# Two held-back second-layer pieces move ahead of the last block's projections

## Chip, cores and metric

One Trainium2 chip, one core. The metric is the device time of one execution in microseconds (us); the figure for a kernel is the median of its runs.

## The reference

One transformer block with adaptive layer norm, one sequence of 2048 rows of 576 numbers, 32 heads of 18:

```
mod = silu(c) @ w_mod                      # six vectors sa, ca, ga, sb, cb, gb
h = layernorm(x) * (1 + ca) + sa
x = x + ga * (softmax(q k^T * 18**-0.5) v) @ wo       # q, k, v = h @ wqkv
h = layernorm(x) * (1 + cb) + sb
x = x + gb * silu(h @ w1) @ w2             # hidden width 4608
```

All inputs and the output are float32.

## The kernel before

The rows are cut into four blocks of 512 (`b` = 0 to 3), and a block into four row tiles of 128 (`j` = 0 to 3). TensorE runs attention block after block; what follows attention in a block, called here its second half, is done while the attention of the next block runs. For the last block there is no next attention: its second half is the tail of the kernel, in which TensorE has nothing else to do. Every product is split into a high and a low part, so that one product is three matmul passes.

`post(b)` (line 1059) writes down the second half of a block as a list of items in the order in which TensorE is to run them: each `fl.add` appends one. TensorE's order is exactly this list's; the other engines' orders (VectorE is DVE, ScalarE ACT, GpSimd POOL, and SyncE, or SP, which issues all transfers named here) are made by a scheduler that walks the same program with a model of durations. So a change in the list can also change the order on DVE and on SP. An engine, SP among them, works through its own order strictly: whatever stands behind a waiting instruction waits too.

The second half of a block is, in order:

1. `o_T` (line 1067): the attention output `ou` is split into `th` and `tl`.
2. The output projection, `proj` (line 1089), row tile after row tile: 28 matmuls of 128x288 into two banks `psp`, one bank per half of the 576 columns. Its weights `wo` lie in the buffers that later hold the first four `w1t` and one `w2t`. When a row tile's two halves are done, `add_x1` (line 1105) adds each bank to the residual tile `x` on DVE (line 1108).
3. The layer norm of that row tile, in four steps (`ln_steps`, line 1143): statistics (lines 1121, 1125, 455), the reciprocal root (line 457 on POOL, lines 463 to 467 on DVE), and the scaling into `ob` (line 471), of which POOL copies a last piece (line 472). For row tile j these steps are strewn among the projections of row tile j + 1; for the last row tile (j = 3) there is no next projection, and they come in the loop at line 1194.
4. `h_T` (line 1146): 20 transposes of `ob` by TensorE (`psT`, line 1157), five column tiles kt of four row tiles each. In the last block they come as 15 transposes of row tiles 0 to 2 and then 5 of row tile 3. From each `psT` bank ACT makes `eq` (line 475) and DVE makes `hh` (line 478), and `hl` = `eq` - `hh` (line 485) on DVE for even kt and on POOL for odd kt.
5. The two layers of the MLP: `mlp1` (line 1234, `ps`<-`hh`,`w1t`, 128x512), and `mlp2` (line 1267, `ps`<-`w2t`,`g`, 128x288), whose results DVE adds to the residual tile; a row tile that has its last addition goes to the output (line 1287).

**Held-back pieces.** Block 2 doesn't finish its second layer before block 3's second half begins: its last four hidden tiles' share of `mlp2` is kept as a list `left` of 32 pieces of three matmuls each. `rest(n)` (line 1173) puts the next n of them into the list of the running block, as work for TensorE while others are busy. The 32 pieces in their order: 16 for the row tiles 0 and 1 of block 2, 8 for row tile 2 (12 matmuls per column half), 8 for row tile 3. After a row tile's last piece DVE adds its second half, and the row tile is written out.

For block 3 `LREST` (line 60) says how many pieces stand ahead of the projections of each row tile, the loop at line 1194 puts two ahead of each of the four layer norm steps of the last row tile, and a `rest(99)` behind the transposes takes what is left.

**The residual tiles.** Residual tiles share five buffers (`x1`, `bufs=5`, line 1056). Block 2 holds four of them until they are written out; block 3's four loads (line 1057) take the fifth buffer and then those of block 2's row tiles 0, 1 and 2, in this order. So the load of block 3's residual tile 3 has to wait until block 2's row tile 2 has been written out.

In the rows below, `x_23433`, `x_23435`, `x_23437`, `x_23439` are block 2's residual tiles 0 to 3; `x_30924`, `x_30926`, `x_30928`, `x_30930` are block 3's.

Of the kernel before, what the change touches and what calls it, by code (L numbers as in the profile page):

```python
# [56 lines left out]
END = -4  # L57
END0 = 40
LP0 = 1000
REST, LREST = (16, 8, 0, 0), (22, 0, 0, 0)  # L60
LP = 8000
PB = 9
ORDER = (
# [346 lines left out]
def tile_adaln_block(ctx: ExitStack, tc: tile.TileContext, x, wqkv, wo, w1, w2, c, ccol, wfirst, wcol, out):  # L410
# [589 lines left out]
    def out_b(i, ov):  # L1000

        b, qd = divmod(i, NQUAD)
        if qd == 0:
            if b:
                fill.until("h_T")
            o[b] = att.tile([P, KT, QB], F32, tag="o", name="ou", bufs=1)
        ou = o[b]
        tt = ou[:, 4, :]
        nc.vector.transpose(tt, ov)
        blocks = tt.rearrange("p (b c) -> p b c", c=32)  # L1010
        rec = att.tile([P, 16], F32, name="rec", bufs=2)
        nc.vector.reciprocal(rec, blocks[:, :, DH])
        nc.vector.tensor_tensor(blocks[:, :, :DH], blocks[:, :, :DH], rec[:, :, None].to_broadcast([P, 16, DH]), op=ALU.mult)
        nc.vector.transpose(ov, tt)
        o["at", b] = None
        chain([("V", 700), ("V", 260), ("V", 460), ("V", 700)], plan.t + 700, None, lambda at: o.update({("at", b): at + (5500 if b else 6500)}))
        for h in range(4):
            for kt, r0, d0, d1 in head_rows(4 * qd + h):
                nc.sync.dma_start(ou[r0:r0 + d1 - d0, kt, :], ov[32 * h + d0:32 * h + d1, :])
        del quads[i]  # L1020
        if qd == NQUAD - 1:
            post(b)
# [36 lines left out]
    def post(b):  # L1059
# [5 lines left out]
        last = state["tail"] = plan.off = b == NQB - 1  # L1065
# [51 lines left out]
        def ln_stat(j, n):  # L1117
            if n == 0:
                c["st", j] = pool.tile([P, 2, 6], F32, name="st6", bufs=3), pool.tile([P, 1, 2], F32, name="mv2", bufs=4)
            st6, mv = c["st", j]  # L1120
            nc.vector.bn_stats(st6[:, n, :], c["x1"][j][:, n * HH:(n + 1) * HH])
            if n == 0:
                plan.op("V", plan.t, 450)
                return
            nc.vector.bn_aggr(mv[:, 0, :], st6)
            c["v", j] = rstd_a(pool, mv, 1)
            c["ve", j] = Event(plan)
            c["x", j].then(lambda at: chain([("V", 450), ("V", 330), ("G", 560)], at, None, c["ve", j].set))

        def ln_rs(j):  # L1130
            c["rs", j] = rstd_b(pool, *c["v", j], 1)
            state["ln"] = False
            c["rs_at", j] = Event(plan)
            c["ve", j].then(lambda at: plan.op("V", at, 770, c["rs_at", j].set))

        def ln_c(j):
            if j == 0:
                c["ob"] = att.tile([P, NST, 640], F32, tag="o", name="ob", bufs=1)
            ln_apply(c["x1"][j], c["ob"][:, j, :], c["st", j][1][:, 0, :], c["rs", j], nc.vector)
            c["ln", j] = Event(plan)  # L1140
            c["rs_at", j].then(lambda at: chain([("V", 540), ("G", 240)], at, None, c["ln", j].set))

        def ln_steps(j):
            return [lambda: ln_stat(j, 0), lambda: ln_stat(j, 1), lambda: ln_rs(j), lambda: ln_c(j)]
# [28 lines left out]
        def rest(n):  # L1173
            for _ in range(min(n, len(left))):
                fl.add(*left.pop(0))
# [9 lines left out]
        for j in range(NST):  # L1185
            rest((REST if not last else LREST)[j])
            steps_ = dict(zip((1, 4, 8, 11), ln_steps(j - 1))) if j else {}
            for part in range(len(GP)):
# [2 lines left out]
                    fl.add(0, lambda i=part // 3: w2_load(i))  # L1191
                if part in steps_:
                    fl.add(0, steps_[part])
        for step in ln_steps(3):
            if b == 0:
                fl.add(700)
            rest(2)
            fl.add(0, step)
        if not last:
            rest(99)  # L1200
# [563 lines left out]
    step = 0  # L1764
# [101 lines left out]
```

## Time and profile before

| | us |
|---|---|
| runs | 2343.11, 2345.21, 2345.0 |
| median | 2345.0 |
| profiled execution, its own time | 2344.63 |
| span of the instructions in its profile | 2342.8 |
| TensorE (PE) matmuls busy, and weight loads (PEld) | 2288.0 and 1581.4 |
| VectorE (DVE) busy | 1764.1 |
| ScalarE (ACT) busy | 1472.2 |
| GpSimd (POOL) busy | 707.8 |

The span runs from the first instruction to the last; the execution's own time has 1.83 us around it. The profile's times are counted from the start of the span. The tail, from the last attention matmul on, begins at 2064.9 and is 278 us long, about an eighth of the span. TensorE is busy in 98% of the span, so what it can gain lies in the places where it waits; "busy" also hides the times at which its granted clock is below full.

### The profile page before, as it was taken

Reading aid. Unit: us, or ns where it says so; the run is one execution under the profiler, and the core shown is the slowest. Engines: PE = TensorE matmul, PEld = TensorE weight load, DVE = VectorE, ACT = ScalarE, POOL = GpSimd, SP = SyncE. Lnnn points to the kernel's source line nnn. Section 1 sums busy time; section 2 is a strip of 40 time slices with the busy share of each in tenths; the row PEclk is TensorE's granted clock in tenths of the full one; section 3 lists DMA queues with packets and bytes.
Section 4 is the critical chain, followed back from the end, with each engine's and each line's share of the span. In section 5 each row is a group of like instructions: output and inputs, shape, how many; then the busy total and the mean of one; then the engine's idle time right before and its main releaser. Section 6 shows DMA issues by size and latency. Waiting matters only on the chain.

```text
span 2342.8 us, 52324 instructions
## 1 busy us (share of the span) xinstructions
PE 2288.0 (98%) x19954; PEld 1581.4 (67%) x19954; DVE 1764.1 (75%) x3080; ACT 1472.2 (63%) x2712; POOL 707.8 (30%) x856
## 2 busy tenths in 40 slices
PE   7999999999899999999999999999999999979999
PEld 6974444444576766776676777667677777668998
DVE  7788899987788888877888888778887787244333
ACT  4347777776577777766677777666777677722121
POOL 4213333316556666765311111122211111110000
PEclk9999999998999999999999999999999999999999
DMA  7555555446556666665655545564555554345553
GB/s 277 175 173 177 181 182 175 158 151 198 187 196 216 212 226 219 220 227 189 219 168 178 173 167 166 177 197 167 183 165 172 186 186 161 110 169 178 218 204 120
DMA packets 201619, 433.55 MB, mean 185 GB/s; under 512 B 31506, under 2 KB 67762, under 8 KB 201370
## 3 DMA queue, kind: packets, MB, share of 16 engines
q1 hardware_dynamic: 201370, 430.21, 55.3%
q8 instruction: 159, 2.61, 0.5%
q14 instruction: 90, 0.74, 0.1%
HBM read 339.07 MB, written 86.33 MB: 182 GB/s over the span
## 4 chain that ended last, share of the span: by engine, by line
PE 89%; DVE 4%; DMA 3%; ACT 1%; POOL 1%; issue 1%; SPq 0%; DVEq 0%; ACTq 0%; POOLq 0%
PE ps L560 27%; PE psv L991 19%; PE psa L902 14%; PE ps L554 10%; PE psb L954 9%; PE psqk L666 3%; DVE mx L904 2%; PE psv L560 1%; PE psp L560 1%; PE psqk L560 1%; PE psv L1552 1%; PE psp L554 1%; DMA ka<-kscr 1%; DMA raw<-in_w 1%; PE psqk L1552 1%
## 5 line engine op out<-in xcount | busy, mean ns | idle before, releaser
L904 DVE TENSOR_REDUCE mx<-psa 128x1 f32<-128x512 f32 x2048 | 1330.0, 685 | 279.5 <-PE psb L954 170.4
L956 ACT ACTIVATE pt<-psb 128x512 f32<-128x512 f32 x2048 | 1148.2, 599 | 469.3 <-PE psb L954 306.0
L954 PE MATMUL psb<-qt,kb 56*128 56x512 f32 x2048 | 743.5, 421 | 4.5 <-ACT pt L956 4.5
L902 PE MATMUL psa<-ka,qt 54*128 54x512 f32 x2016 | 732.9, 417 | 11.0 <-DVE mx L904 9.1
L902 PEld LDWEIGHTS psa<-ka,qt 54*128 54x128 f32 x2016 | 347.9, 186 | 304.3 <-DVE mx L904 168.4
L991 PE MATMUL psv<-pt,vt 128*32 128x512 f32 x4096 | 512.2, 606 | 0.3 <-ACT ov L995 0.3
L560 PE MATMUL ps<-w2t,g 64*128 64x288 f32 x4992 | 412.5, 293 | 1.6 <-POOL w2t L787 1.0
L560 PEld LDWEIGHTS ps<-w2t,g 64*128 64x128 f32 x4992 | 384.8, 185 | 42.2 <-DVE x L1108 6.0
L954 PEld LDWEIGHTS psb<-qt,kb 56*128 56x128 f32 x2048 | 351.8, 186 | 29.0 <-ACT pt L956 18.1
L560 PE MATMUL ps<-hh,w1t 64*128 64x512 f32 x1944 | 351.5, 394 | 0.0
L1264 POOL TENSOR_TENSOR g<-etmp,g 128x512 fp32r<-128x512 f32 x108 | 137.8, 1296 | 386.9 <-ACT g L1263 349.6
L991 PEld LDWEIGHTS psv<-pt,vt 128*32 128x32 f32 x4096 | 102.5, 109 | 212.2 <-issue 204.5
L560 PEld LDWEIGHTS ps<-hh,w1t 64*128 64x128 f32 x1944 | 193.9, 186 | 44.0 <-ACT etmp L1260 3.4
L1115 POOL TENSOR_TENSOR x<-x,gt 128x288 f32<-128x288 f32 x116 | 92.9, 801 | 388.1 <-ACT gt L1114 383.3
L560 PE MATMUL ps<-hl,w1t 64*128 64x512 f32 x864 | 177.4, 391 | 0.0
L1108 DVE TENSOR_TENSOR x<-ps,x 128x288 f32<-128x288 f32 x184 | 83.1, 453 | 105.0 <-PE ps L554 69.8
L554 PE MATMUL ps<-w2t,g 128*128 128x288 f32 x960 | 130.2, 296 | 0.0
L554 PEld LDWEIGHTS ps<-w2t,g 128*128 128x128 f32 x960 | 129.1, 189 | 1.5 <-issue 0.8
L1260 ACT ACTIVATE eq<-ps 128x512 f32<-128x512 f32 x36 | 21.5, 600 | 146.6 <-PE ps L554 146.6
L554 PE MATMUL ps<-hh,w1t 128*128 128x512 f32 x360 | 107.1, 391 | 0.0
L560 PEld LDWEIGHTS ps<-hl,w1t 64*128 64x128 f32 x864 | 88.4, 186 | 15.2
L1261 DVE SCALAR_TENSOR_TENSOR etmp<-etmp 128x512 f32<-128x512 f32 x108 | 75.8, 742 | 11.8 <-ACT etmp L1260 10.9
(157 smaller groups left out, 2126.5 us busy)
## 6 DMA issues: line engine op xcount, KB each, us to landing
w1t<-w1s SPq DMA_DIRECT2D x108, 640.0 KB
w2t<-w2s SPq DMA_DIRECT2D x108, 576.0 KB
kb<-kscr SPq DMA_DIRECT2D x512, 108.0 KB
ka<-kscr SPq DMA_DIRECT2D x504, 108.0 KB
w1s<-w1t SPq DMA_DIRECT2D x36, 640.0 KB
w2s<-w2t SPq DMA_DIRECT2D x36, 576.0 KB
vt<-vscr SPq DMA_DIRECT2D x32, 608.0 KB
qt<-qscr SPq DMA_DIRECT2D x128, 108.0 KB
```

Of the source, the lines that this page charges most:

```text
L554: mm(self.ps[late], lhsT=lhsT, rhs=rhs, start=(i == 0), stop=(i == self.n - 1))
L560: done = mm(self.ps[g], lhsT=lhsT[rows], rhs=rhs[rows], start=(s == 0), stop=(s == self.end))
L666: mm(qk_ps[0], lhsT=w[b][:, kt, :], rhs=(hTl if a else hTh)[:, kt, n * 512:(n + 1) * 512], start=(i == 0), stop=(i == 13))
L902: mm(ps, lhsT=t["q"][64 * j:64 * j + 54, hp, stt * P:(stt + 1) * P], rhs=t["a" if ("a", kc, hp) in t else "b", kc, hp][64 * j:64 * j + 54, ...
L904: return lambda: nc.vector.tensor_reduce(t["mx"][:, 2 * j + hp, stt, kc:kc + 1], ps, axis=AX.X, op=ALU.max)
L954: state["pe"] = mm(ps, lhsT=t["b", kt // 4, hp][64 * e:64 * e + 56, kt % 4 * P:(kt % 4 + 1) * P], rhs=t["q"][64 * e:64 * e + 56, hp, :], s ...
L956: nc.scalar.activation(t["P"][kt, hp][:, e, :], ps, AF.Exp, scale=SCALE)
L991: mm(t["ps"][32 * h:32 * h + 32, :], lhsT=t["v"][:, c0:c0 + 32], rhs=t["P"][kt, h // 2][:, h % 2, :], start=(kt == 0), stop=(kt == NKT - 1 ...
L1108: nc.vector.tensor_add(c["x1"][j][:, hs], ps, c["x1"][j][:, hs])
L1115: nc.gpsimd.tensor_add(c["x1"][j][:, hs], c["x1"][j][:, hs], t)
L1261: nc.vector.scalar_tensor_tensor(t, t, 1.0, u, op0=ALU.add, op1=ALU.mult)
L1264: (nc.vector if last else nc.gpsimd).tensor_tensor(g[:, 1, :], t, f(g[:, 0, :]), op=ALU.subtract)
```

## The change

```
-REST, LREST = (16, 8, 0, 0), (22, 0, 0, 0)
+REST, LREST = (16, 8, 0, 0), (24, 0, 0, 0)
...
-        for step in ln_steps(3):
+        for n, step in enumerate(ln_steps(3)):
             if b == 0:
                 fl.add(700)
-            rest(2)
+            rest(1 if last and n else 2)
             fl.add(0, step)
```

For the last block, 24 of the 32 pieces stand ahead of the projections instead of 22. Ahead of the last row tile's four layer norm steps stand 2, 1, 1 and 1 pieces, five in all; before there were 2 each, which is eight by the code and by the order (the change's own words say seven). Behind the transposes three pieces are left instead of two: 24 + 5 + 3 = 32, as 22 + 8 + 2 before. No instruction of TensorE is added or taken away.

On TensorE, the stretch from the end of the last projection (`psp`) to the first layer of the MLP; `ps_31031` is the second column half of block 2's row tile 2, `ps_31242` and `ps_31243` (now `ps_31239` and `ps_31240`) the halves of its row tile 3:

```order
 L554 MATMUL psp<-wo_30920,tl 128x288
 L554 MATMUL psp<-wo_30922,th 128x288 x2
-L554 MATMUL ps_31031<-w2t,g 128x288 x6
-L554 MATMUL ps_31242<-w2t,g 128x288 x12
-L554 MATMUL ps_31243<-w2t,g 128x288 x6
+L554 MATMUL ps_31239<-w2t,g 128x288 x12
+L554 MATMUL ps_31240<-w2t,g 128x288 x3
 L1157 MATMUL psT<-ident,ob 128x128 x20
-L554 MATMUL ps_31243<-w2t,g 128x288 x6
+L554 MATMUL ps_31240<-w2t,g 128x288 x9
```

The six last matmuls of `ps_31031` have gone from here to the place ahead of the first projection; 15 matmuls are left between the last projection and the transposes where 24 were, and 9 instead of 6 stand behind the transposes.

On SP, the transfers from the loads of the residual tiles 1 and 2 of block 3 to the writing of block 2's last row tile; `w1t` and `w2t` are the weights of the MLP's first hidden tiles:

```order
 L1057 DMA x_30926<-in_x 128x576
 L1057 DMA x_30928<-in_x 128x576
+L1287 DMA out<-x_23437 128x576
+L1057 DMA x_30930<-in_x 128x576
 L744 DMA w1t<-w1s 128x1280 x4
-L744 DMA w2t<-w2s 128x1152
-L1287 DMA out<-x_23437 128x576
-L744 DMA w2t<-w2s 128x1152 x2
-L1057 DMA x_30930<-in_x 128x576
-L744 DMA w2t<-w2s 128x1152 x2
+L744 DMA w2t<-w2s 128x1152 x5
 L1287 DMA out<-x_23439 128x576
```

The writing of block 2's row tile 2 and the load of block 3's residual tile 3 stood behind the four `w1t` loads, and now stand ahead of them.

On DVE, the additions around the last row tile's layer norm, before:

```order
L471 TENSOR_SCALAR ob<-x_30928,mv_31188,rs 128x576
L1108 TENSOR_TENSOR x_23437<-ps_31031,x_23437 128x288
L1108 TENSOR_TENSOR x_23439<-ps_31242,x_23439 128x288
L1108 TENSOR_TENSOR x_30930<-psp,x_30930 128x288 x2
L1121 BN_STATS st_31239<-x_30930 128x6 x2
L1125 BN_AGGR mv_31240<-st_31239 128x2
L455 TENSOR_SCALAR ve<-mv_31240 128x1
```

and now:

```order
L1108 TENSOR_TENSOR x_30930<-psp,x_30930 128x288
L471 TENSOR_SCALAR ob<-x_30928,mv_31197,rs 128x576
L1121 BN_STATS st_31247<-x_30930 128x6
L1125 BN_AGGR mv_31248<-st_31247 128x2
L1108 TENSOR_TENSOR x_23439<-ps_31239,x_23439 128x288
L455 TENSOR_SCALAR ve<-mv_31248 128x1
```

The two additions to `x_30930` no longer stand behind the additions of block 2's pieces: the first comes while the last projections run (ahead of these rows), the second is the first row here. The addition of `ps_31239` now stands within the last row tile's layer norm, and in the same way that of `ps_31240` now stands between the first two `hh` (line 478) and the first `hl` (line 485), where before one `hh` and one `hl` more stood ahead of it. The second addition to `x_23437`, which was in the rows of before, now follows line 1087, ahead of the first addition to `x_30924`.

## Prediction

> **What bounds the kernel now.** I read first the chain of waits in order of time, cut to the tail (start, length, what). Outside the tail it is TensorE almost throughout and the change touches nothing there; in the tail it leaves TensorE for 17 us:
>
> ```profile
> 2064.86 8.95 PE ps L554 x66
> 2073.81 14.86 PE psp L554 x112
> 2088.66 0.81 PE ps L554 x6
> ...
> 2089.49 0.47 DVE x L1108
> ...
> 2089.98 8.93 DMA out<-x
> ...
> 2098.97 3.48 DMA x<-in_x
> ...
> 2102.53 0.82 DVE x L1108 x2
> ...
> 2106.58 1.33 PE psT L1157 x5
> 2107.91 231.49 PE ps L554 x1374
> ```
>
> The 66 matmuls are the 22 pieces ahead of the projections, the 112 the projections. The six at 2088.66 finish block 2's row tile 2; its addition, its writing (8.93 us) and then the load of the last residual tile into the same buffer (3.48 us) follow one another, and only then can the last layer norm begin. Behind 2107.91 the chain is TensorE to the end, so what is won ahead of that is won at the end.
>
> Next the timeline of TensorE over the same place (start, length, line; in brackets idle time and what ended it):
>
> ```profile
> 2088.50 3.35 PE L554 MATMUL ps<-w2t,g 128*128 128x288 f32 x24
> 2091.68 1.47 PE L1157 MATMUL psT<-ident,ob 128*128 128x128 f32 x12
> 2103.13 0.88 PE L1157 MATMUL psT<-ident,ob 128*128 128x128 f32 x3 [9.98 <-DVE x L1108]
> 2106.58 1.33 PE L1157 MATMUL psT<-ident,ob 128*128 128x128 f32 x5 [2.58 <-DVE ob L471]
> 2107.56 1.79 PE L554 MATMUL ps<-w2t,g 128*128 128x288 f32 x6
> 2109.15 1.05 PE L554 MATMUL ps<-hh,w1t 128*128 128x512 f32 x2
> 2110.09 0.80 PE L554 MATMUL ps<-hl,w1t 128*128 128x512 f32 x1
> 2111.54 0.62 PE L554 MATMUL ps<-hh,w1t 128*128 128x512 f32 x2
> 2112.22 0.62 PE L554 MATMUL ps<-hh,w1t 128*128 128x512 f32 x2
> ```
>
> TensorE has idled 9.98 + 2.58 us here. It is also slow afterwards: six matmuls of 128x288 take from 2107.56 to 2109.15, 0.265 us each, against 8.95 / 66 = 0.135 in the chain. The windows view says why (third number from the end: granted clock):
>
> ```profile
> 2094.00:2096.00 2.00, 0.00 (x0) 0.00 (x0) 0.00 (x0) 0.00 (x0) 0.00 (x0) 1.00 1.00 300
> 2096.00:2098.00 2.00, 0.00 (x0) 0.00 (x0) 0.00 (x0) 0.00 (x0) 0.00 (x0) 0.84 0.99 392
> 2098.00:2100.00 2.00, 0.00 (x0) 0.00 (x0) 0.00 (x0) 0.00 (x0) 0.00 (x0) 0.50 1.04 424
> 2110.00:2111.00 1.00, 1.00 (x3) 0.81 (x3) 1.00 (x3) 0.78 (x1) 1.00 (x1) 0.50 0.92 359
> 2111.00:2112.00 1.00, 1.00 (x6) 0.77 (x5) 1.00 (x3) 0.78 (x1) 0.18 (x1) 1.00 0.84 327
> ```
>
> The last transposes before the wait end at 2091.68 + 1.47 = 2093.15. A mean of 0.84 over 2096 to 2098 puts the fall to 0.50 at about 2097.4, 4.2 us later. The clock is back at about 2111, 4.4 us after work resumed at 2106.58.
>
> **The change, step by step.** Times stay on the axis of before.
>
> *Pieces ahead.* Two pieces are 6 x 0.135 = 0.81 us, so the last projection ends at 2088.66 + 0.81 = 2089.47. That alone is a shift and no cost: the same matmuls are missing later.
>
> *The residual load.* When does the last residual tile arrive now? DVE and SP of before:
>
> ```profile
> 2075.82 0.68 DVE L1087 TENSOR_TENSOR th<-ou,th 64x512 fp32r<-64x512 f32 x1 [2.32 <-ACT th L1082]
> ```
>
> ```profile
> 2073.79 0.88 SPq L1287 DMA_DIRECT2D out<-x  x2
> 2075.97 1.13 SPq L1057 DMA_DIRECT2D x<-in_x  x2
> 2087.22 2.07 SPq L744 DMA_DIRECT2D w1t<-w1s  x4
> ```
>
> The 24th piece ends at 2073.81 + 0.81 = 2074.6, but its addition stands behind line 1087 on DVE: 2076.5 + 0.46 = 2077.0. The round trip that follows is bounded by two measured ones: a row tile written without a crowd let SP go on after 2075.97 - 2073.79 = 2.18 us; behind the weights it took 8.93. I take 2.18, since the first weights follow only at 2087.22. With 3.48 for the load the tile is there at 2082.7; with 8.93, at 2089.4. The first addition needs it when the first half of the last projection is done, 14.86 / 8 = 1.86 us ahead of 2089.47, at 2087.6. So the wait goes wholly by the first price, and comes back by 1.8 us at most by the second. SP waits in this round trip, and the four `w1t` stand behind it: until 2079.2, or 2085.9 by the dear price, while their buffers come free at 2087.22 + 0.81 = 2088.03. Nothing waits for that.
>
> *The last layer norm.* What is late next is this chain. Row tile 2's layer norm in before shows it without a DMA wait, with the `ob` of the row tile before it in between, as it will now be for row tile 3:
>
> ```profile
> 2084.99 0.46 DVE L1108 TENSOR_TENSOR x<-psp,x 128x288 f32<-128x288 f32 x1 [0.28 <-PE psp L554]
> 2085.36 0.57 DVE L471 TENSOR_SCALAR ob<-x,mv,rs 128x576 f32<-128x576 f32 x1
> ...
> 2086.33 0.21 DVE L1125 BATCH_NORM_AGGREGATE mv<-st 128x2 f32<-128x12 f32 x1
> 2086.58 0.15 DVE L455 TENSOR_SCALAR ve<-mv 128x1 f32<-128x1 f32 x1
> ...
> 2088.16 0.58 DVE L471 TENSOR_SCALAR ob<-x,mv,rs 128x576 f32<-128x576 f32 x1
> ...
> 2107.91 1.53 DVE L478 TENSOR_SCALAR hh<-psT,modc 128x512 fp32r<-128x512 f32 x2 [1.38 <-ACT eq L475]
> 2109.35 0.68 DVE L485 TENSOR_TENSOR hl<-eq,hh 128x512 fp32r<-128x512 f32 x1
> ```
>
> From the addition to the end of `ob`: 2088.16 + 0.58 - 2084.99 = 3.75 us. The inserted addition can start when 12 matmuls of `ps_31239` are done, 2089.47 + 12 x 0.135 = 2091.09, just as DVE comes free (2089.50 + 1.34 + 0.21 = 2091.05); the next instruction starts 0.37 later (as from 2084.99 to 2085.36), so line 455 starts at 2091.48, where it could have at 2091.09: 0.39 us. `ob` ends at 2089.50 + 3.75 + 0.39 = 2093.64. Meanwhile TensorE has 15 matmuls (2.03 us) and 15 transposes at (1.47 - 0.27) / 11 = 0.109 us, taking 0.27 as one's own length (1.64 us): busy to 2093.14. The last five transposes start at 2093.69, with 0.55 us of idling.
>
> *From the transposes to the first layer.* ACT:
>
> ```profile
> 2107.10 2.12 ACT L475 ACTIVATE eq<-psT,modc 128x512 f32<-128x512 f32 x3 [31.31 <-PE psT L1157]
> ```
>
> In before ACT followed the first transpose by 0.52 us at half clock; at full clock I take 0.35 (an estimate: the transpose itself halves from about 0.5 us). So `eq` at 2094.04, `hh` 0.81 later at 2094.85 (as 2107.10 to 2107.91), and `hl` 1.44 after that (2107.91 to 2109.35) plus 0.37 for the addition of `ps_31240` now ahead of it: 2096.66, done 0.68 later at 2097.34, and its matmul 0.06 behind (2110.03 to 2110.09): 2097.40. TensorE has ready work ahead of that only to 2096.11: five transposes to 2094.24, nine matmuls to 2095.46, two on `hh` from 2095.66 (2094.85 + 0.81) at 0.227 us, from (2112.22 - 2111.54) / 3. So 0.20 and 1.29 us of idling stay at this place. The moved piece behind the transposes is covered by this same wait and costs nothing; without that cover it would cost 0.41.
>
> *The clock.* From the first `hl` matmul to the one that starts at 2111.54 in before are four matmuls in 1.45 us; at full clock 4 x 0.227 = 0.91. That is 0.54 us more, if the clock stays up. The idle stretches left, 0.55, 0.20 and 1.29 us, are all shorter than the 2.85 us from 2093.15 to 2096.00 that left the clock at 1.00.
>
> [...]
>
> *Weights.* In before the first `w1t` had 22 us to arrive (2087.22 to 2109.15); now they are needed at 2095.66, 7.6 after their issue. The sizes, from the list of transfers:
>
> ```profile
> w1t<-w1s SPq DMA_DIRECT2D x8, 640.0 KB
> w2t<-w2s SPq DMA_DIRECT2D x5, 576.0 KB
> ...
> out<-x SPq DMA_DIRECT2D x4, 288.0 KB
> ```
>
> In before the written row tile, with four `w1t` and one `w2t` ahead of it, landed at 2098.91, 11.7 us after the first `w1t` was issued. If transfers are served one after another, the first two are there after 1280 / 3424 of that, 4.4 us: at 2092.4, no cost. If all progress together, as late as 2099.7, and the `hl` matmul waits to 2099.7 + 0.45, 2.75 us later. I take the first: the written tile was the last issued and landed last, which speaks for service in turn.
>
> **Sum.** 2110.09 - 2097.40 = 12.69 us, and 0.54 for the clock: 13.2 us. The profiled execution's 2344.63 becomes 2331.4 and its span 2342.8 becomes 2329.6. The median of the three runs is 0.4 us above the profiled execution: 2345.0 - 13.2 = 2331.8.
>
> **Rivals.**
>
> *The clock falls again.* Three short idle stretches within 4 us might count as one. Against it: each is under the 2.85 us that did no harm. For it: nothing here shows several together. Price: 4.4 us at half clock, half of it lost, 2.2 us: 2334.0. [...]
>
> *The weights become the wait*, as priced: 13.2 - 2.75 = 10.5 us of gain, 2334.5.
>
> *Slower.* The load now ahead of `w1t` on SP stalls the weights: SP doesn't issue them until the row tile is written. This decides only if the writing takes more than 2088.03 - 2077.0 = 11 us, and the kernel is slower by 0.2% only if it takes 11 + 13.2 + 4.7 = 29 us: 2349.7 or more. The dearest writing seen here is 8.93, in a crowd that isn't there at 2077.
>
> *The change doesn't do what it says*, that is, the load doesn't come earlier, or a wait as long takes its place: 2345. The order of SP speaks against the first; for the second I find no candidate but the weights.
>
> **How the numbers follow.** The forecast has 0.80, the clock rival 0.07, the weights rival 0.07, no gain 0.04, slower 0.02. The first three are faster. About 0.2% (4.7 us) is what a measurement of this kernel can tell from no change. Faster 0.94, within 0.2% 0.04, slower 0.02. The low end: in before, TensorE needed 30 x 0.135 + 20 x 0.109 + 6 x 0.227 = 7.6 us for what it did between 2088.66 and 2111.54, so at most 22.9 - 7.6 = 15.3 us can go: 2329.7, and 0.7, a third of the 2.1 us between the runs shown, for the spread: 2329.0. The high end takes in either milder rival, and the same 0.7: 2335.2.
>
> **What would show it.** Right: SP writes a row tile near 2077 and loads one near 2079; DVE shows no wait for a residual load; TensorE waits about 0.6 us for `ob` of row tile 3 and about 1.3 for the first `hl`; granted clock 1.00 from 2090 to 2110; first `hl` matmul near 2097.4; span near 2329.6. Wrong: a long wait of DVE for the load, a clock of 0.50 after 2095, TensorE waiting for `w1t`, or the first `hl` matmul after 2100.

## The result, and the profile after

The changed kernel takes 2332.2 us (median of 6 runs, 2329.92 to 2338.06) where the kernel before, measured beside it, takes 2345.14 (6 runs, 2343.11 to 2347.39). The ratio is 0.9947, with a 95% interval of 0.9934 to 0.9961: 9.1 to 15.5 us won. The profiled execution of the changed kernel happens to be its slowest, 2338.06 us with a span of 2336.3, so it stands only 6.6 us below the profiled execution of before. The chain of waits shows why its total misleads (start, length, what):

```profile
2068.81 9.74 PE ps L554 x72
2078.55 14.86 PE psp L554 x112
2093.41 1.61 PE ps L554 x12
...
2097.00 0.59 DVE ob L471
...
2097.63 0.34 PE psT L1157
...
2098.00 0.79 ACT eq L475
...
2098.82 1.53 DVE hh L478 x2
2100.34 0.36 DVE x L1108
2100.71 1.54 DVE hl L485
...
2102.29 230.53 PE ps L554 x1366
...
2332.85 0.46 DVE x L1108
```

The tail, from the first piece ahead of the projections to the last addition, begins at 2068.81, where it began at 2064.86 before: 3.95 us were lost ahead of it, in code that is the same in both. The tail itself lasts 2333.31 - 2068.81 = 264.50 us, against 275.02 (2064.86 to 2339.88) before. So 10.5 us are won in the tail. The two DMA rows of the chain, writing and load, are gone, and what stands between the last projection and the first layer now is the layer norm alone: the addition of `ps_31239` that now stands inside it, `ob`, transposes, `eq`, `hh`, the addition of `ps_31240`, `hl`.

In the queue of SP the order is the new one (start, length, line):

```profile
2079.93 1.13 SPq L1057 DMA_DIRECT2D x<-in_x  x2
2081.16 0.38 SPq L1287 DMA_DIRECT2D out<-x  x1
2085.64 0.33 SPq L1057 DMA_DIRECT2D x<-in_x  x1
2091.97 2.25 SPq L744 DMA_DIRECT2D w1t<-w1s  x4
```

The row tile is written from 2081.16, and 4.48 us later its buffer is loaded with the last residual tile; both stand ahead of the weights. DVE's list of waits over 2060 to 2120 no longer has a row of `x` waiting for `in_x`. Before, it had one of 11.0 us (us in total, times, longest):

```profile
DVE x L1108 <- DMA x<-in_x: 11.0, 1, 11.0
```

TensorE's timeline over the same place (in brackets idle time and what ended it):

```profile
2097.63 0.77 PE L1157 MATMUL psT<-ident,ob 128*128 128x128 f32 x5 [0.59 <-DVE ob L471]
...
2102.29 0.51 PE L554 MATMUL ps<-hl,w1t 128*128 128x512 f32 x1 [1.88 <-DVE hl L485]
2102.64 0.63 PE L554 MATMUL ps<-hh,w1t 128*128 128x512 f32 x2
...
2103.49 1.05 PE L554 MATMUL ps<-hh,w1t 128*128 128x512 f32 x2
```

Of the idle stretches of 9.98 and 2.58 us there remain 0.59 and 1.88. But two matmuls of 128x512 take 0.63 us at 2102.64 and 1.05 at 2103.49. The windows say what that is (third number from the end: granted clock):

```profile
2102.00:2103.00 1.00, 0.71 (x3) 0.62 (x4) 0.96 (x3) 0.65 (x1) 0.00 (x0) 1.00 1.02 419
2103.00:2104.00 1.00, 1.00 (x5) 0.76 (x4) 1.00 (x2) 0.80 (x2) 0.00 (x0) 0.57 1.04 429
2104.00:2105.00 1.00, 1.00 (x4) 0.81 (x3) 1.00 (x2) 0.00 (x0) 0.51 (x1) 0.50 1.05 410
...
2106.00:2107.00 1.00, 1.00 (x5) 0.76 (x4) 0.32 (x1) 0.00 (x0) 0.00 (x0) 0.72 1.05 394
```

By the means of 0.57 and 0.72 the clock falls to a half at 2103.14 and is back at 2106.56: 3.4 us, after the idling is over and with TensorE busy all the time.

### The profile page after: what moved, and what is told of

It reads as the page before. It is cut to its first block, busy times and chain, and to the rows that moved or that the text cites. A ratio compares the mean times of both kernels' runs of the same rounds, so it can differ in the third digit from the quotient of the medians.

```text
span 2336.3 us, 52325 instructions
## 1 busy us (share of the span) xinstructions
PE 2288.4 (98%) x19954; PEld 1584.9 (68%) x19954; DVE 1764.9 (76%) x3080; ACT 1472.7 (63%) x2712; POOL 707.6 (30%) x856
## 4 chain that ended last, share of the span: by engine, by line
PE 87%; DVE 5%; DMA 3%; POOL 1%; ACT 1%; issue 1%; SPq 0%; DVEq 0%; ACTq 0%; POOLq 0%
PE ps L560 27%; PE psv L991 19%; PE psa L902 14%; PE ps L554 10%; PE psb L954 8%; PE psqk L666 3%; DVE mx L904 2%; DMA raw<-in_w 1%; PE psp L560 1%; PE psv L560 1%; PE psv L1552 1%; PE psp L554 1%; DMA qt<-qscr 1%; PE psqk L560 1%; PE psqk L1552 1%
## 5 line engine op out<-in xcount | busy, mean ns | idle before, releaser
L1261 DVE SCALAR_TENSOR_TENSOR etmp<-etmp 128x512 f32<-128x512 f32 x108 | 74.6, 730 | 11.8 <-ACT etmp L1260 10.9
```

Of the source, the lines that this page charges most:

```text
L1261: nc.vector.scalar_tensor_tensor(t, t, 1.0, u, op0=ALU.add, op1=ALU.mult)
```

## The experiments

The theory is that of the prediction: the last residual tile comes into the buffer of block 2's row tile 2, and the 24th piece is the one that frees it early; the whole gain is that wait. Its main rival is that pieces ahead of the projections are worth something each. Beside it two remainders were to be explained, the first `hl` matmul and the clock.

All readings of the tail stand in one table here, worked out as above from each profiled execution's chain and TensorE timeline: the tail's length, the time from the end of the last projection to the first `hl` matmul, and from that to the end of TensorE's last piece.

| kernel (execution) | tail, us | to first `hl` | from there | clock |
|---|---|---|---|---|
| before (1st, 2nd, 3rd) | 275.02, 275.01, 274.61 | 21.43 (1st) | 229.31 (1st), 228.92 (3rd) | fell |
| changed (1st) | 264.50 | 8.88 | 230.53 | fell |
| changed (2nd) | 264.45 | 8.88 | 230.48 | fell |
| changed (3rd) | 262.88 | 8.88 | 228.91 | stayed |
| ahead_only | 263.53 | 7.95 | 230.48 | fell |
| hl1_dve | 261.99 | 7.96 | 228.95 | stayed |
| xpt | 261.55 | 8.32 | 228.94 | stayed |
| xpt_20 | 260.98 | 7.93 | 228.91 | stayed |
| xpt_20_hl | 261.30 | 7.92 | 229.25 | stayed |
| p26 (1st) | 262.60 | 7.81 | 228.89 | stayed |
| p26 (2nd) | 264.24 | 7.81 | 230.53 | fell |
| p23 | 275.47 | - | - | fell |

### 23 pieces instead of 24 (p23)

```
-REST, LREST = (16, 8, 0, 0), (24, 0, 0, 0)
+REST, LREST = (16, 8, 0, 0), (23, 0, 0, 0)
```

> 23 pieces ahead instead of 24, five behind the last projection, four behind the transposes. Theory (the gain is the residual buffer's): row tile 2 of block 2 lacks one piece, so its writing and the load of the last residual tile fall behind the weights again. DVE waits about 10 us for the load, the clock falls to 0.50, and the time is within 0.2% of the kernel before (2341 to 2347). Rival (the gain comes from where the pieces stand, some 6 us for each piece moved ahead): about half the gain, 2338 to 2340, with no long wait of DVE.

Measured: 2345.82 us (10 runs), ratio to before 1.0 [0.9991, 1.0009]. Its chain has the old pair of transfers again:

```profile
2066.17 9.34 PE ps L554 x69
2075.51 14.86 PE psp L554 x112
2090.37 0.41 PE ps L554 x3
...
2091.67 8.96 DMA out<-x
...
2100.65 2.66 DMA x<-in_x
```

So does DVE's list of waits:

```profile
DVE x L1108 <- DMA x<-in_x: 10.6, 1, 10.6
```

The three matmuls left at 2090.37 are the one piece on which the row tile's writing, and with it the load, still hangs. One piece of the two is worth nothing; the gain comes whole with the 24th. That is a step, as a buffer makes it, and no price for each piece.

### The kernel before without the buffer's wait, no piece moved (xpt)

The kernel before, with the last residual tile in an idle buffer of its own (one of the attention's `pt`, which line 956 writes), loaded at the start of the last `post`; the pieces stay at 22, eight and two.

```
-        for j in range(NST):
+        for j in range(NST - (b == NQB - 1)):
...
-        c = ready[b]
+        c = ready[b]; b == NQB - 1 and (c["x1"].append(pts[0].rearrange("p a b -> p (a b)")[:, :D]), nc.sync.dma_start(c["x1"][3], x[b * QB + 3 * P:b * QB + 4 * P, :D]))
```

> The kernel before, with its 22 + 8 + 2 pieces as they were, but the last residual tile of block 3 lies in a buffer of its own (one of attention's, free by then), so that its load waits for no writing. Theory (the gain is the residual buffer's alone): nearly the whole gain without moving a piece; DVE has no wait for a load; the first hl matmul comes about 8.6 us after the last projection, and the tail, from the first held-back matmul to the last addition (275.0 us before, 264.5 in the changed kernel), is 261.8 us if the clock stays up and 263.4 if it falls, that is 2330 to 2335. Rival (the pieces must stand ahead): 2340 or more.

Measured: 2328.78 us (5 runs, 2327.97 to 2331.7), the kernel before, measured beside it, 2344.9; ratio 0.9933 [0.992, 0.9945]. Its chain:

```profile
2061.67 8.95 PE ps L554 x66
2070.62 14.86 PE psp L554 x112
2085.47 3.18 PE ps L554 x24
2088.65 1.76 PE psT L1157 x16
...
2093.80 228.94 PE ps L554 x1366
...
2322.76 0.46 DVE pt L1108
```

66 matmuls ahead and 24 behind, as before, and the whole gain without moving a piece: the tail is 261.55 us. The layer norm of the last row tile is out of the chain, since 24 matmuls behind the last projection cover it where the changed kernel's 15 leave 0.59 us. This and p23 together show the cause of the gain: the end of the wait for the buffer, and not the place of the pieces.

### Only the first half of the change (ahead_only)

24 pieces ahead, and two instead of one at each of the last layer norm's later steps, as before:

```
-            rest(1 if last and n else 2)
+            rest(2)
```

> Only the first half of the change: 24 pieces ahead, and two ahead of each of the last layer norm steps as before, so that all eight that are left stand between the last projection and the transposes, and none behind them. Theory (the gain is the residual buffer's): the whole gain is there, 2330 to 2333. By the chain the last five transposes start 4.9 us after the last projection (TensorE's own work, 24 matmuls and 15 transposes, is now longer than the layer norm), the addition of the second half leaves the place ahead of hl, DVE's hl starts ahead of POOL's and takes 0.7 us, and the first hl matmul comes 8.2 us after the last projection, 0.6 earlier than in the changed kernel. Rival (the second half of the change is needed too): slower than the changed kernel by over 1 us, since nothing covers the time between transposes and hh.

Measured: 2333.84 us (5 runs, 2330.29 to 2336.8), ratio 0.9954 [0.9941, 0.9966]; the changed kernel, measured beside it: 2332.09 (5 runs, 2330.06 to 2333.52), ratio 0.9944 [0.9931, 0.9956]. Its timeline of all engines (POOL is GpSimd):

```profile
2096.48 0.73 PE L554 MATMUL ps<-hh,w1t 128*128 128x512 f32 x2 [1.28 <-DVE hh L478]
2097.06 0.68 DVE L485 TENSOR_TENSOR hl<-eq,hh 128x512 fp32r<-128x512 f32 x1
2097.22 1.66 POOL L485 TENSOR_TENSOR hl<-eq,hh 128x512 fp32r<-128x512 f32 x1 [2.54 <-DVE hh L478]
...
2097.79 0.50 PE L554 MATMUL ps<-hl,w1t 128*128 128x512 f32 x1 [0.58 <-DVE hl L485]
```

TensorE waits 1.28 us for `hh` and 0.58 for `hl`, 1.86 in all, where the changed kernel waits 0.59 and 1.88. DVE's `hl` takes 0.68 us here. The first `hl` matmul comes 7.95 us after the last projection, 0.93 earlier than in the changed kernel. The second half of the change isn't needed for the gain; the time is a little above the 2330 to 2333 expected. Whether the second half costs anything in total time stays open, since the intervals lie over each other. In the profiles, with the clock fallen in both, the tail without it is 1 us shorter (263.53 against 264.50).

### The second `hl` on VectorE (hl1_dve)

In the changed kernel DVE and GpSimd work on an `hl` each at the same time. The timeline of that kernel, all engines:

```profile
2100.26 0.45 DVE L1108 TENSOR_TENSOR x<-ps,x 128x288 f32<-128x288 f32 x1
2100.43 1.26 POOL L485 TENSOR_TENSOR hl<-eq,hh 128x512 fp32r<-128x512 f32 x1 [2.54 <-DVE hh L478]
2100.63 1.61 DVE L485 TENSOR_TENSOR hl<-eq,hh 128x512 fp32r<-128x512 f32 x1
```

The addition at 2100.26, of `ps_31240`, has put DVE's `hl` 0.2 us behind GpSimd's. DVE's takes 1.61 us. In before it started 0.17 ahead of GpSimd's and took 0.68; the timeline of before has for GpSimd:

```profile
2109.52 1.66 POOL L485 TENSOR_TENSOR hl<-eq,hh 128x512 fp32r<-128x512 f32 x1 [2.69 <-DVE hh L478]
```

There GpSimd is the slow one. To test that this is the loss, `hl` of the second column tile (kt = 1) goes to DVE too:

```
-            mod_lo(kt, hi, c["hl"][:, kt, :] if kt < 4 else None, tmp, nc.vector if last and kt % 2 == 0 else nc.gpsimd)
+            mod_lo(kt, hi, c["hl"][:, kt, :] if kt < 4 else None, tmp, nc.vector if last and (kt % 2 == 0 or kt == 1) else nc.gpsimd)
```

> The changed kernel with the second hl (kt = 1) on DVE instead of POOL. Theory (POOL's hl, which starts 0.2 us ahead of DVE's, holds DVE's up): DVE's first hl takes 0.7 us instead of 1.6, the first hl matmul comes 7.9 us after the last projection instead of 8.9, TensorE waits about 1 us for it instead of 1.9, and the time is 0.5 to 2.5 us under the changed kernel's, the upper end if the clock then stays up. Rival (DVE's hl is slow by itself here, from the transfers that fill the memory at this time or from its place): it takes 1.6 us again and nothing is won.

Measured: 2330.11 us (5 runs, 2326.94 to 2335.38), ratio 0.9944 [0.993, 0.9958]. Its timeline:

```profile
2092.03 0.69 DVE L485 TENSOR_TENSOR hl<-eq,hh 128x512 fp32r<-128x512 f32 x1
...
2092.77 0.50 PE L554 MATMUL ps<-hl,w1t 128*128 128x512 f32 x1 [0.95 <-DVE hl L485]
```

Without GpSimd beside it the same instruction, in the same order on DVE, takes 0.69 us. TensorE waits 0.95 instead of 1.88, and the tail is 261.99 us. The loss of 0.93 was the neighbour's. In total time the two kernels aren't told apart.

### The changed kernel again, and before again

Does the clock fall because of the idle stretches, or not in every execution? Both kernels ran again unchanged, and each was profiled twice more.

> The changed kernel once more, to see which of its rows stay from one execution to the next. Theory (the chain sets it): the chain from the end of the last projection to the first matmul on hl is the same again, 8.9 us, with 0.6 us of waiting for ob and 1.9 us for hl, and DVE's first hl takes 1.6 us again because POOL's hl starts ahead of it. [...] The time: 13 us under the kernel before either way, give or take 2.

> The changed kernel a third time. If the idle stretches set the clock's fall (0.6 and 1.9 us within 5 us), it falls again between 0.3 and 1 us after the first hl matmul and the tail is 264.5 us. If the phase of a window that runs freely sets it, one of three executions may miss it: 262.9 us then.

> The kernel before, once more, for its rows. Two things are open: whether its tail is 275.0 us in every execution, and where its tail begins (2064.9 us in the first profile; the changed kernel's two executions have 2068.8 and 2062.9). Theory (what is ahead of the tail varies by execution and not by kernel): a start between 2060 and 2069, a tail of 275.0 within 0.3. Rival (the change also shortens what is ahead of the tail, by some 2 us): a start of 2065 or more here and in the next.

> The kernel before a third time. Theory (what is ahead of the tail varies by execution and not by kernel): a start of the tail between 2060 and 2069, a tail of 275.0 within 0.3. Rival (the change also shortens what is ahead of it): a start of 2065 or more.

Measured: 2332.09 (its five runs above), 2334.76, 2342.69 and 2347.79 us. In the changed kernel's third execution TensorE's idle stretches are the same as in its first:

```profile
2095.94 0.77 PE L1157 MATMUL psT<-ident,ob 128*128 128x128 f32 x5 [0.59 <-DVE ob L471]
...
2100.59 0.51 PE L554 MATMUL ps<-hl,w1t 128*128 128x512 f32 x1 [1.88 <-DVE hl L485]
```

Its chain is not:

```profile
2100.59 228.91 PE ps L554 x1366
```

The clock stays at 1.00, in all windows up to 2108, and the same 1366 matmuls take 228.91 instead of 230.53 us. The fall costs 1.6 us and comes in two of the three profiled executions, with the same idle stretches of 0.59 and 1.88 us in all three. In before the third execution has 228.92 behind the first `hl` matmul instead of 229.31, the clock being back ahead of that matmul.

What goes with it can be read from the traces, though no run was made for it. In the records of the granted clock of all fourteen profiles every change of the clock lies on a grid of 3.413 us, whose place differs from one execution to the next: each stretch at one clock, but for the last, which the profile's end cuts off, lasts a whole multiple of 3.413 us, up to 1252.69 us. In the changed kernel's first execution one step of this grid runs from 2099.73 to 2103.14 (first number behind the comma: TensorE's busy time):

```profile
2099.73:2103.14 3.41, 1.53 (x6) 0.96 (x7) 3.38 (x5) 1.18 (x3) 1.26 (x1) 1.00 1.02 414
```

In the third execution the steps lie so:

```profile
2096.19:2099.61 3.42, 2.43 (x16) 1.76 (x14) 2.49 (x4) 2.12 (x3) 0.88 (x1) 1.00 1.01 410
2099.61:2103.02 3.41, 2.42 (x11) 2.00 (x12) 3.38 (x5) 1.45 (x2) 0.61 (x2) 1.00 1.03 415
```

In the first, all of the 1.88 us of idling (2100.41 to 2102.29) is in one step, and the clock falls where the step ends. In the third the same idling (2098.71 to 2100.59) is split between two steps, and the clock stays. The other tails, up to 2320 us, agree: eight steps at full clock with at most 1.59 us of busy time are each followed by a fall, and no step with 1.72 or more is. The two executions of the 26 pieces below differ in the same way, 1.83 us (2091.70 to 2095.11) in the one that stays up and 1.59 (2097.73 to 2101.14) in the one that falls. This holds for these tails alone. In the attention of the changed kernel the clock also falls behind a step in which TensorE is busy throughout, with matmuls of 54 to 56 rows (529.59 to 533.01).

An estimate follows for the changed kernel. If the grid can lie anywhere, it holds the 1.88 us whole within one step in 3.41 - 1.88 = 1.53 of 3.41 us of its places, and the fall is to be expected in about half of the executions.

The tail's start is at 2064.86, 2062.94 and 2068.43 in before and at 2068.81, 2062.90 and 2067.11 in the changed kernel. What stands ahead of the tail moves by 6 us from one execution to the next in both, which is most of the scatter of the totals; no profile shows that the change shortened it.

### 26 pieces (p26)

```
-REST, LREST = (16, 8, 0, 0), (24, 0, 0, 0)
+REST, LREST = (16, 8, 0, 0), (26, 0, 0, 0)
```

> 26 pieces ahead instead of 24, five behind the last projection, one behind the transposes. Theory (the 24th piece is a step, and behind it the layer norm's chain is the bound, so that each further piece ahead only takes cover away, 0.41 us each): tail 0.8 us longer than the changed kernel's 264.5, the clock falls as there. Rival (more pieces ahead is better): shorter.

> The kernel with 26 pieces ahead again, whose clock stayed at 1.00 although TensorE idled 0.5, 1.3 and 0.6 us within 4 us. If the phase of the window decides, the clock may fall here: tail 264.1 instead of 262.6. If the lengths decide (no stretch over 1.3 us), it stays up: 262.6 again.

Measured: 2330.15 us (4 runs), ratio 0.9935 [0.9922, 0.9949], and 2336.06 in one more execution; tails of 262.60 and 264.24 us. The loss that I expected for p26 from shorter cover did not come. The first execution's timeline:

```profile
2091.47 0.46 DVE L1108 TENSOR_TENSOR x<-ps,x 128x288 f32<-128x288 f32 x1 [1.25 <-PE ps L554]
...
2093.28 0.68 DVE L485 TENSOR_TENSOR hl<-eq,hh 128x512 fp32r<-128x512 f32 x1
...
2093.44 1.67 POOL L485 TENSOR_TENSOR hl<-eq,hh 128x512 fp32r<-128x512 f32 x1 [2.92 <-DVE hh L478]
...
2094.02 0.50 PE L554 MATMUL ps<-hl,w1t 128*128 128x512 f32 x1 [0.58 <-DVE hl L485]
```

With the addition ahead of both `hh`, DVE's `hl` starts 0.16 ahead of GpSimd's and takes 0.68. That gives back what the cover lost, and the first `hl` matmul comes 7.81 us after the last projection. The clock stayed up in the first execution and fell in the second, though TensorE's idle stretches are 0.47, 1.27 and 0.58 us in both. A window of the second execution, with a clock of 0.50:

```profile
2102.00:2104.00 2.00, 2.00 (x6) 1.55 (x5) 1.97 (x3) 0.18 (x1) 1.28 (x1) 0.50 1.06 428
```

### An own buffer and fewer pieces ahead (xpt_20 and xpt_20_hl)

The buffer of xpt with 20 pieces ahead of the projections, added to the changed kernel, and then the second `hl` on DVE as well:

```
-REST, LREST = (16, 8, 0, 0), (24, 0, 0, 0)
+REST, LREST = (16, 8, 0, 0), (20, 0, 0, 0)
...
-            rest(1 if last and n else 2)
+            rest(1 if last and n > 1 else 2)
```

> A buffer of its own for the last residual tile, and 20 pieces ahead, six behind the last projection (2, 2, 1, 1), six behind the transposes, so that TensorE has work in each of the three waits of the changed kernel. Theory (what is left is idling between the projections and the first hl, and the fall of the clock that it brings): idling of about 0.5 us in all instead of 2.5, no fall of the clock, first hl matmul 7.95 us after the last projection, which comes 1.6 us earlier than in the changed kernel; tail 260.4 us, 4.1 under the changed kernel's, time 2328 or so. Rival (the clock falls with the weights' transfers or the phase of its window, not with the idling): the fall is there again and the tail is 261.9 or more.

> The same with the second hl on DVE. Theory (only the order of the starts matters for the two hl, and DVE's starts first here anyway): as without it, within 0.3 us: tail 260.4. Rival (POOL's hl costs DVE something in any case): 0.3 to 1 us less.

Measured: 2330.69 us, ratio 0.9939 [0.9926, 0.9951], and 2329.46, ratio 0.9945 [0.993, 0.9959]. TensorE's waits from 2060 to 2110 in xpt_20 (engine, line, waited for: us in total, times, longest):

```profile
PE psp L554 <- DVE th L1087: 0.4, 1, 0.4
PE psT L1157 <- DVE ob L471: 0.2, 1, 0.2
```

Its tail, 260.98 us, is the shortest of all: more pieces behind the last projection cover `ob` but for 0.2 us, at the price of 0.4 within the first projection (up to 2075.23), which 20 pieces no longer bring late enough for `th`. That 0.4 is most of the 0.6 by which the tail misses the expected 260.4. With the second `hl` on DVE the tail is 0.3 longer, since TensorE then waits a second time, for that `hl` (2095.86), and DVE has both to make. In total time neither is told apart from xpt, which has the lowest median, or from the changed kernel.

## Why the prediction was right, and where it was off

The forecast was 2331.8 us and the median is 2332.2. By its steps:

- *The load's wait.* Right, and shown by p23 and xpt. The round trip on SP was priced at 2.18 us with 8.93 as the other bound; it took 4.48, behind two loads of residual tiles issued right ahead of it, and what made it longer isn't shown. The load was issued at 2085.64, and with the 3.48 of before it would be there at 2089.1, ahead of the 2091.5 at which its first addition is needed (1.86 ahead of 2093.41). The weights were issued 13.4 us after the start of the first projection in both kernels (2073.81 to 2087.22, 2078.55 to 2091.97), and no wait for them shows in TensorE's rows.
- *The last layer norm.* Right: transposes 4.22 us after the last projection (2093.41 to 2097.63), as forecast, with 0.59 us of idling for 0.55. `eq`, `hh` and the addition come in the forecast distances, and `hl` starts 7.22 us after the last projection, forecast 7.19.
- *The first `hl`.* The term that was mis-sized: "done 0.68 later". It took 1.61, because the addition that I had counted at 0.37 also let GpSimd begin first. The first `hl` matmul came at 8.88 us instead of 7.93: 0.95 us lost. I had taken the duration from a row in which DVE had been first.
- *The clock.* The second term that was mis-sized. It was to stay up, worth 0.54 us, since each idle stretch was under 2.85. It fell in two executions of three, and the tail behind the first `hl` matmul took 230.53 us where 229.31 - 0.54 = 228.8 were forecast: 1.7 us. This was the rival with a chance of 0.07 and a price of 2.2; the price was near, the chance much too low, and a clock of 0.50 was a sign of being wrong that the prediction itself had named. That no single stretch is long was the wrong reason. In these tails the falls go with how much TensorE idles within one step of 3.41 us (each came behind at most 1.59 us of busy time, none behind 1.72 or more), and with the stretches as they came the chance was about a half by the estimate above. Nor is the 0.54 there in every execution of before: in the third the clock was back ahead of the first `hl` matmul.
- *The sum.* 13.2 us were forecast for the tail, and 10.5 came in the profiled execution: 13.2 - 0.95 - 1.7. In the third execution, with the clock up, it was 275.02 - 262.88 = 12.1, and hl1_dve, in which neither loss occurs, has a tail of 261.99 where 275.0 - 13.2 = 261.8 was forecast. The mean over three executions of each kernel is 274.88 - 263.94 = 10.9 us, within the interval of 9.1 to 15.5; the medians differ by 12.9. That the median comes within 0.4 us of the forecast is luck in part, since 2 us of the difference aren't the tail's. These 2 us stay open: the starts of the tail scatter too widely in the profiles to show a difference, but in all seven kernels without the wait the medians differ by more than the tails do (in xpt by 16.1 against 13.3).
- *The rivals.* Weights as the wait, no gain and slower: none of them shows.

The kernels in which no stretch was over 0.95 us (hl1_dve, xpt, xpt_20 and xpt_20_hl) kept the clock, with one profile each. The least busy steps of hl1_dve and xpt have 2.46 us of busy time, far from the 1.59 behind which it fell.

## What to carry to other kernels

When a load waits at the end of a program, look for what last used its buffer: a step between two settings of a number with nothing won by the first (p23) is the sign of a buffer that comes free, and a buffer of its own then brings the same gain without moving work. When an instruction is put ahead of another that has a neighbour on GpSimd, ask which of the two then starts first: here DVE's `hl` took 0.68 us where it started ahead of GpSimd's and 1.61 where it started behind it. A forecast that meets the total can still miss two of its terms: compare the stretch that the change touches, where 6 us of scatter ahead of it don't reach. And for short idle stretches like these, ask how much of 3.41 us they take together (behind a step with 1.59 us of busy time the clock fell here, behind one with 1.83 it stayed up), and expect that two executions of one kernel can differ, as the tails of 264.45 and 262.88 us do.

## What the runs showed of the hardware

**Two engines on the same kind of instruction.** For the 128x512 `hl` (line 485), the engine that started first took as long as with no `hl` of the other beside it, and the other took longer. GpSimd first by 0.2 us: 1.26 on GpSimd (1.27 at 2104.49, with no `hl` on DVE), 1.61 on DVE (0.69 in hl1_dve, with none on GpSimd), whose instruction ends 0.55 us after GpSimd's (2101.69 to 2102.24). DVE first by 0.16 to 0.17: 0.68 on DVE, 1.66 on GpSimd. The next `hl` of DVE in ahead_only, p26 and xpt, which starts while GpSimd's is under way, takes 0.93 to 0.94 us and ends 0.54 to 0.55 after it too. What holds up the second isn't shown.

**The clock after short idle stretches.** In the changed kernel's first execution it fell to a half with TensorE busy again, about 0.9 us after the second of two stretches of 0.59 and 1.88 us (2097.04 to 2102.29), stayed there for 3.4 us (2103.14 to 2106.56) and cost 1.6 (230.53 against 228.91 for the same 1366 matmuls); with the same stretches it stayed up in the third execution. The changes of the clock lie on a grid of 3.413 us in all fourteen profiles, and in these tails the falls come behind steps of it with at most 1.59 us of busy time. In the changed kernel, ahead_only and p26 TensorE was busy for 1.44 to 1.59 us in those steps.
